# Attention with a two-layer FFN: the second layer summed in six PSUM banks over a pair of token tiles, the first layer's block products in two

## The chip, the core and the metric

The kernel runs on one core of a Trainium2 chip. The metric is the device time of one execution in microseconds; before the change its median over three runs is 757.24 us (756.86 to 758.57).

## What is computed

Attention for 4 batches, 8 heads, 576 positions and head size 64, with a bias from a small network on the log of the distance; then an FFN over the 2304 tokens.

```python
scores = q @ k^T / 8 + bias(rel. position)
attn   = softmax(scores);  x = (attn @ v)            # -> 2304 x 512
h = x @ w_in                                          # 512 -> 2048
g = maximum(0.01 * h, h)
out = g @ w_out                                       # 2048 -> 512
```

`w_in` and `w_out` arrive as float64. The kernel gets them as pairs of 32-bit words and builds float32 from the bits on the chip.

## The kernel before

The program has two stages, both with an order of work written out by hand (`manual_schedule`): each engine takes its instructions strictly in the order in which the Python code emits them, and waits on semaphores that the framework puts in. So a waiting instruction holds up all that is emitted behind it on its engine.

**Attention** is a sequence of 16 units (two heads of one batch), each of nine tiles: `step(n)` issues scores (TensorE), softmax (DVE and ScalarE), transposes and the product with v. In fixed slots of each unit (L577) it also takes one operation from `early_ops`: the weights of the FFN are cut in 16 chunks `m`, each with a half of `w_in` (h = 0) and a half of `w_out` (h = 1), and one half is assembled by `w_abs` (ScalarE, absolute value of the raw word) and four `w_bits` (DVE). A raw half is 512 KB; `w_fill` issues its load on SP's queue as soon as one of the `raw` buffers is free, and a buffer becomes free at the fourth `w_bits` of its half. `EARLY` chunks are assembled in attention, the rest in the first pair of the FFN, from the list `conv`, where each half's four `w_bits` are followed by the `w_abs` of the half after next.

**The FFN** runs over 24 periods `g`: three pairs of 384-token tiles (`p`), each with eight groups `m` of two weight chunks. The period `g` computes the first layer of its group with seven block products instead of eight, after Winograd: `prod(g, j)` multiplies a sum of blocks of `w_in` (`w1b`, built by `s_sum`, `w1_hi`, `w1_lo`) with a sum of blocks of x (`xo`, built by `x_sum`, `x_hi`, `x_lo`). Every operand is split into a high part in the fast format and a rest (`_hi` on ScalarE, `_lo` a subtraction), and a product is six matmuls of 384 columns: high by high, high by rest and rest by high, for two halves of the contraction. `keep` (ScalarE) and `comb` (DVE) add the products in `c` tiles to the four blocks of h; `relu` (two ScalarE operations) and `g_lo` make the high part and the rest of g. Later groups keep their built weights in DRAM: `w1_out` writes 1792 KB in the first pair, `w1_in` reads them back in the two others.

In the same period `l2(g-1, q)`, q = 0 to 5, multiplies the previous group's g with `w_out` (`ws`, built by `w2_split`), six matmuls of 512 columns each, in a bank of tag `o`; `flush` then adds the bank to the result in `xa`, on DVE, and after the pair's last group sends the rows out. The order on TensorE in one period is: products 0 and 1, l2 0, product 2, l2 1, product 3, l2 2, product 4, l2 3, l2 4, products 5 and 6, l2 5.

PSUM has eight banks: tag `s` has two tiles of two banks each, tags `t` and `o` two tiles of one bank. Products 0 and 1 share one `s` tile, 2 and 3 the other, 4 to 6 take turns in `t`, and l2 has `o`.

```python
def prod(g, j):
    if j in (0, 2):
        t = pstile("s")
        bank[g, j], bank[g, j + 1] = t[:, 0:HT], t[:, 512:512 + HT]
    elif j > 3:
        bank[g, j] = pstile("t")[:, 0:HT]
```

GpSimd does `s_sum`, `w1_lo`, the rest part of `w2_split`, `x_sum`, and `g_lo` for blocks 0 and 3; DVE does `g_lo` for blocks 1 and 2, the flushes and the assembly of weights. `work(budget)` puts, at four places of a period, some of the waiting weight operations into the order: first those of `todo` (next group's weights), then `conv`, until the given costs are used up.

Of the kernel before, what the change touches and what calls it, by code (L numbers as in the profile page):

```python
# [8 lines left out]
F32 = mybir.dt.float32  # L9
# [14 lines left out]
KW = 2 * S + 64  # L24
EARLY = 9
RING = 7
HT = 384
NG = MF // 2
# [12 lines left out]
def attention_ffn(ctx: ExitStack, tc: tile.TileContext, qt, kt, vm, vt, wi, wo, cst, out):  # L41
# [330 lines left out]
    pools, y1, y2, raws, w1b, ws, st_, xt = {}, {}, {}, {}, {}, {}, {}, {}  # L372
    free, nxt = [3], [0]

    def w_fill():
        while nxt[0] < 2 * MF and free[0]:
            p = nxt[0]
            free[0] -= 1
            t = pools["raw"].tile([128, DM, 2], I32, tag="raw", name="raw", bufs=3)
# [50 lines left out]

    def w1_lo(g, k):
        s, y = w1_src(g, k)
        w = w1b[g % 2]
        nc.gpsimd.tensor_sub(w[:, 1, s], y, w[:, 0, s].bitcast(F32))
        if k == 2:
            del y1[2 * g], y1[2 * g + 1]
# [7 lines left out]
    def w1_ops(g):  # L444
        l = [(0.01, s_sum, g, k) for k in range(4)]
        for k in range(3):
            l += [((0.65, 0.36, 1.05)[k], w1_hi, g, k), (0, w1_lo, g, k)]
        return l + [(0, w1_out, g)]

# [14 lines left out]
    def x_sum(p, o):  # L464
        t = pools["raw"].tile([128, DM, 2], I32, tag="raw", name="raw", bufs=3) if p else pools["fp"].tile([128, 2, DM], F32, tag="ws", name="ws", bufs=4)
# [8 lines left out]
    def x_hi(p, o):  # L474
        x_new(p, o)
        nc.scalar.copy(out=xo[p, o][:, 0], in_=x_of(p, o))
# [3 lines left out]

    bank, gt, gf, ct, flush_q = {}, {}, {}, {}, []

    def prod(g, j):
        if j in (0, 2):
            t = pstile("s")
            bank[g, j], bank[g, j + 1] = t[:, 0:HT], t[:, 512:512 + HT]
        elif j > 3:
            bank[g, j] = pstile("t")[:, 0:HT]
        w, x = w1b[g % 2], xo[g // NG, j]
        n = 0  # L490
        for k in range(2):
            c = slice(128 * k, 128 * k + 128)
            for a, b in ((0, 0), (0, 1), (1, 0)):
                nc.tensor.matmul(bank[g, j], w[:, a, PROD[j], c], x[:, b, k, :], start=(n == 0), stop=(n == 5))  # L494
                n += 1

    def c_new(g, c):
        ct[g, c] = pools["fp"].tile([128, HT], F32, tag="c", name="c", bufs=6)
# [16 lines left out]
    def g_lo(g, c):  # L515
        t = gt[g, c]
        (nc.vector if c in (1, 2) else nc.gpsimd).tensor_sub(t[:, 1], gf.pop((g, c))[:], t[:, 0].bitcast(F32))  # L517

    def l2(g, q):
        tk = (q + 3) % 6  # L520
        o = pstile("o")
        n = 0
        for i in range(2):
            t, w = gt[g, 2 * i + tk // 3], ws[2 * g + i]
            c = slice(128 * (tk % 3), 128 * (tk % 3) + 128)
            for a, b in ((0, 0), (0, 1), (1, 0)):
                nc.tensor.matmul(o[:], t[:, a, c], w[:, b], start=(n == 0), stop=(n == 5))  # L527
                n += 1
        flush_q.append((g, tk, o))

    def flush():
        if not flush_q:
            return
        g, tk, o = flush_q.pop(0)
        p, m = divmod(g, NG)
        t0 = 2 * HT * p
        y = xa[tk // 3][:, :, t0 + 256 * (tk % 3):t0 + 256 * (tk % 3) + 256]
        o = o[:].rearrange("p (a c) -> p a c", a=2)
        if m:
            nc.vector.tensor_add(y, o, y)  # L540
        else:
            nc.vector.tensor_copy(y, o)
        if m == NG - 1:
            t0 += 128 * tk
            nc.sync.dma_start(out=out[t0:t0 + 128, :].rearrange("t (a c) -> t a c", a=2), in_=y)

    with tc.manual_schedule():
# [6 lines left out]
        for n in range(NTILE + LAG + 6):  # L554
# [15 lines left out]
            if n == 13:  # L570
                w_fill()
                for m in range(EARLY):
                    for h in range(2):
                        early_ops += [(w_abs, m, h)] + [(w_bits, m, h, k) for k in range(4)]
                    if m == 1:
                        early_ops += [f[1:] for f in w1_ops(0)]
            for _ in range({0: 3, 4: 3, 8: 1}.get(i, 0) if n >= 14 else 0):  # L577
                if early_ops:
# [18 lines left out]
        fp.tile([128, HT], F32, tag="gf", name="gf", bufs=2)  # L597
        fp.tile([128, HT], F32, tag="c", name="c", bufs=6)
        for m in range(EARLY, MF):
            y2[m] = fp.tile([128, DM], F32, name=f"y2_{m}")  # L600
        for o in (0, 1):
            x_hi(0, o)
            x_lo(0, o, nc.gpsimd)
        for o in (3, 2, 4, 6):
            x_sum(0, o)
        for o in (2, 3, 4, 5, 6):
            x_hi(0, o)
        for o in (2, 3, 4, 5, 6):
            x_lo(0, o, nc.vector)

        halves_ = [(m, i) for m in range(EARLY, MF) for i in range(2)]
# [5 lines left out]
        todo = []  # L617

        def work(budget):
            for l, left in ((todo, 0.8), (conv, budget)):  # L620
                while l and left > 0 and (l[0][1] != w_abs or l[0][3] or len(y1) < RING):
                    cost, f, *args = l.pop(0)
                    f(*args)
                    left -= cost

        G = NG * NPAIR
        for g in range(G + 1):
            p, m = divmod(g, NG)
            a, b = g < G, g > 0
            last = m == NG - 1 and p + 1 < NPAIR  # L630
            todo += [(0.62, w2_split, 2 * g + i) for i in range(2)] if a else []
            if g + 1 < NG:
                while any(t[1:4] == (w_bits, 2 * g + 3, 0) for t in conv):
                    conv[0][1](*conv.pop(0)[2:])
                todo += w1_ops(g + 1)
            elif g + 1 < G:
                w1_in(g + 1)
            if m == NG - 2 and p + 1 < NPAIR:
                todo += [(0, x_hi, p + 1, 0), (0.93, x_lo, p + 1, 0, nc.vector)]

# [11 lines left out]

            def xs(f, *o):
                if last:
                    for i in o:
                        f(p + 1, i)

            def xl(*o):
                if last:
                    for i in o:  # L660
                        x_lo(p + 1, i, nc.vector)

            pr(0)
            do(keep)
            pr(1)
            flush()
            xs(x_sum, 3)
            xs(x_hi, 1)
            lt(0)
            pr(2)  # L670
            do(comb, 2, 2, 0)
            do(comb, 0, 1, 0)
            do(relu, 0)
# [36 lines left out]
            xs(x_hi, 5, 6)  # L710
            xl(4)
            work(0.6)
            do(g_lo, 1)
            do(g_lo, 2)
            xl(5, 6)
            while todo:
                work(0)
            if g == NG - 2:
                assert not conv
            if not a:  # L720
                while flush_q:
                    flush()

# [41 lines left out]
```

## Time and profile before

| what | before |
|---|---|
| median of 3 runs | 757.24 us |
| time of the profiled execution | 760.83 us |
| its span, first to last instruction | 759.0 us |
| TensorE busy | 695.9 us (92%) |
| DVE busy | 546.6 us (72%) |
| ScalarE busy | 405.8 us (53%) |
| GpSimd busy | 312.7 us (41%) |
| mean granted TensorE clock | 0.973 |

The profiled execution's time is 3.6 us above the median of the runs; its span is 1.8 us above it. A span in the rows below is counted in microseconds from the first instruction. Busy time of TensorE has modelled ends, so that a busy TensorE need not be at its peak; the view of one period's chain shows what each product takes when nothing holds it.

Attention ends near 304 us. The FFN's first product starts there; its first pair (periods 0 to 7) takes until about 472, the second until 602 and the third to the end.

### The profile page before, as it was taken

Reading aid. Unit: us, or ns where it says so; the run is one execution under the profiler, and the core shown is the slowest. Engines: PE = TensorE matmul, PEld = TensorE weight load, DVE = VectorE, ACT = ScalarE, POOL = GpSimd, SP = SyncE. Lnnn points to the kernel's source line nnn. Section 1 sums busy time; section 2 is a strip of 40 time slices with the busy share of each in tenths; the row PEclk is TensorE's granted clock in tenths of the full one; section 3 lists DMA queues with packets and bytes.
Section 4 is the critical chain, followed back from the end, with each engine's and each line's share of the span. In section 5 each row is a group of like instructions: output and inputs, shape, how many; then the busy total and the mean of one; then the engine's idle time right before and its main releaser. Section 6 shows DMA issues by size and latency. Waiting matters only on the chain.

```text
span 759.0 us, 11958 instructions
## 1 busy us (share of the span) xinstructions
PE 695.9 (92%) x4240; PEld 560.0 (74%) x4240; DVE 546.6 (72%) x1112; ACT 405.8 (53%) x874; POOL 312.7 (41%) x297
## 2 busy tenths in 40 slices
PE   7999999999999999468888888899999989999997
PEld 3446787787877777457677677788888878888886
DVE  8986888788988896548989969554555765554554
ACT  8996877787787787343344443332233432332331
POOL 0023436554343441566777776222223632222231
PEclk9999999999999999789999999899999999999999
DMA  9987685687479511024343316343322234333202
GB/s 241 352 275 198 186 249 144 204 222 208 136 204 237 160 57 56 0 97 153 140 173 122 143 66 223 128 141 156 113 98 97 98 134 143 106 144 140 97 2 83
DMA packets 36028, 112.35 MB, mean 148 GB/s; under 512 B 8576, under 2 KB 13312, under 8 KB 32896
## 3 DMA queue, kind: packets, MB, share of 16 engines
q1 hardware_dynamic: 35968, 111.59, 45.9%
q8 instruction: 33, 0.54, 0.3%
q14 instruction: 27, 0.22, 0.1%
HBM read 81.28 MB, written 30.29 MB: 147 GB/s over the span
## 4 chain that ended last, share of the span: by engine, by line
PE 48%; DVE 9%; ACT 4%; POOL 3%; issue 3%; ACTq 0%; POOLq 0%; DVEq 0%
PE ps_o L527 21%; PE ps_s L494 13%; PE ps_t L494 7%; PE ps_o L346 2%; DVE c L506 2%; PE ps_s L246 2%; PE ps_t L311 2%; DVE x L540 2%; ACT c L502 1%; DVE y L398 1%; POOL ws L469 1%; DVE y L400 1%; DVE xo L479 1%; DVE y L396 1%; ACT g L512 1%
## 5 line engine op out<-in xcount | busy, mean ns | idle before, releaser
L527 PE MATMUL ps_o<-ws,g 128*128 128x512 f32 x864 | 226.7, 403 | 11.8 <-DVE x L540 7.4
L527 PEld LDWEIGHTS ps_o<-ws,g 128*128 128x128 f32 x864 | 163.7, 193 | 43.8 <-DVE x L540 8.4
L512 ACT ACTIVATE g<-c 128x384 fp32r<-128x384 f32 x96 | 50.3, 524 | 244.8 <-DVE c L506 240.8
L453 POOL TENSOR_TENSOR ws<-y,ws 128x512 fp32r<-128x512 f32 x48 | 65.0, 1375 | 233.5 <-ACT ws L452 228.0
L269 DVE CUSTOM_DVE_ANT_0 p<-ps_s,bias 128x576 f32<-128x576 f32 x128 | 95.0, 751 | 24.0 <-PE ps_s L246 18.6
L277 ACT ACTIVATE p<-p,mx 128x576 f32<-128x576 f32 x128 | 99.7, 779 | 9.8 <-DVE mx L269 7.7
L506 DVE TENSOR_TENSOR c<-ps_s,c 128x384 f32<-128x384 f32 x72 | 40.1, 557 | 88.8 <-PE ps_s L494 88.0
L540 DVE TENSOR_TENSOR x<-ps_o,x 128x512 f32<-128x512 f32 x126 | 86.1, 684 | 20.5 <-PE ps_o L527 20.4
L327 ACT COPY PT<-ps_t 128x512 f32<-128x512 f32 x128 | 73.7, 576 | 43.6 <-PE ps_t L311 43.6
L246 PE MATMUL ps_s<-ks,qs 128*128 128x288 f32 x480 | 93.7, 317 | 1.8 <-DVE mx L269 1.8
L494 PE MATMUL ps_s<-xo,w1a 128*128 128x384 f32 x288 | 63.5, 359 | 23.5 <-ACT c L502 22.8
L246 PEld LDWEIGHTS ps_s<-ks,qs 128*128 128x128 f32 x480 | 67.6, 189 | 15.6 <-issue 7.4
L494 PEld LDWEIGHTS ps_s<-xo,w1a 128*128 128x128 f32 x288 | 54.6, 202 | 31.6 <-ACT c L502 26.7
L311 PE MATMUL ps_t<-ident,p 128*128 128x128 f32 x512 | 77.5, 274 | 0.0
L494 PE MATMUL ps_s<-xo,w1c 128*128 128x384 f32 x288 | 62.1, 350 | 15.1 <-ACT c L502 10.5
L211 POOL TENSOR_TENSOR qs<-raw,qs 64x512 fp32r<-64x512 f32 x30 | 37.8, 1281 | 89.6 <-DVE qs L199 75.5
L346 PE MATMUL ps_o<-PT,v 128*64 128x288 f32 x512 | 69.2, 412 | 0.9 <-DVE PT L301 0.9
L494 PEld LDWEIGHTS ps_s<-xo,w1c 128*128 128x128 f32 x288 | 52.3, 194 | 23.0 <-ACT c L502 14.5
L311 PEld LDWEIGHTS ps_t<-ident,p 128*128 128x128 f32 x512 | 61.1, 140 | 9.0 <-issue 8.2
L506 DVE TENSOR_TENSOR c<-ps_t,c 128x384 f32<-128x384 f32 x96 | 50.5, 551 | 21.6 <-PE ps_t L494 21.6
L517 POOL TENSOR_TENSOR g<-gf,g 128x384 fp32r<-128x384 f32 x48 | 53.0, 1104 | 2.4 <-ACT gf L513 2.4
L287 POOL COPY rb<-sm 128x256 f32<-128x256 f32 x32 | 14.4, 450 | 94.8 <-DVE sm L284 94.8
(106 smaller groups left out, 1130.4 us busy)
## 6 DMA issues: line engine op xcount, KB each, us to landing
w1a<-w SPq DMA_DIRECT2D x8, 1792.0 KB, 7.4
w1c<-w SPq DMA_DIRECT2D x8, 1792.0 KB, 7.4
raw<-kt SPq DMA_DIRECT2D x32, 304.0 KB, 6.0
raw<-qt SPq DMA_DIRECT2D x32, 288.0 KB, 4.5
raw<-wi SPq DMA_DIRECT2D x16, 512.0 KB, 3.7
raw<-wo SPq DMA_DIRECT2D x16, 512.0 KB, 4.0
w<-w1a SPq DMA_DIRECT2D x4, 1792.0 KB, 5.7
w<-w1c SPq DMA_DIRECT2D x4, 1792.0 KB, 6.6
```

The costliest lines, as they stand in the source:

```text
L246: nc.tensor.matmul(s_[:, S0 + HS * hh:S0 + HS * hh + HS], qs[:, c0:c0 + 128], ks[:, k0 + HS * hh:k0 + HS * hh + HS], start=(j == 0), stop= ...
L269: nc.vector.tensor_tensor_reduce(out=p, in0=s_[:, S0:S0 + S], in1=bt, scale=-0.125, scalar=3.4e38, op0=ALU.add, op1=ALU.min, accum_out=i)
L277: nc.scalar.activation(out=p, in_=p, func=AF.Exp, bias=i, scale=-1.0, accum_out=sm)
L311: nc.tensor.transpose(t0[:, 128 * jb:128 * jb + 128], p[:, p0 + 128 * jb:p0 + 128 * jb + 128], ident[:])
L327: nc.scalar.copy(out=PT[:, g, 0:8, c].rearrange("p (j h) c -> p j h c", h=2)[:, :, h, :], in_=t0[:].rearrange("p (j c) -> p j c", j=4))
L346: nc.tensor.matmul(o[64 * h:64 * h + 64, 0:HS], l, r, start=(jb == 0), stop=(jb == 4))
L453: nc.gpsimd.tensor_sub(t[:, 1], y2[c % MF][:], t[:, 0].bitcast(F32))
L494: nc.tensor.matmul(bank[g, j], w[:, a, PROD[j], c], x[:, b, k, :], start=(n == 0), stop=(n == 5))
L506: nc.vector.tensor_add(a if c == src else c_new(g, c), bank[g, j], a)
L512: nc.scalar.activation(out=t[:, 0], in_=h, func=AF.Prelu, alpha=0.01)
L527: nc.tensor.matmul(o[:], t[:, a, c], w[:, b], start=(n == 0), stop=(n == 5))
L540: nc.vector.tensor_add(y, o, y)
```

## The change

- `l2` no longer has a bank of its own for each use. In a pair it keeps six banks: both `s` tiles (q = 0 to 3) and both `o` tiles (q = 4, 5), and accumulates there over the pair's eight groups. `flush` is gone; after the pair's last group each bank is copied out once, by DVE for even q and by ScalarE for odd q.
- All products take turns in the two `t` banks, except in the very first period, where they take `s`, `s`, `o`, `o`, `t`, `t`, `s`.
- The order on TensorE in a period becomes strictly alternating from product 1 on: products 0 and 1, l2 0, product 2, l2 1, product 3, l2 2, product 4, l2 3, product 5, l2 4, product 6, l2 5.
- Ten chunks are assembled in attention instead of nine, with one slot more in each unit, and group 1's `s_sum` too; the rest of group 1's weights is built before the first period. `conv` starts with period 1 and has six chunks.
- The `raw` buffers are two instead of three; the `y1` ring has eight tiles, `c` eight.
- `g_lo` of all blocks and `w1_lo` (but for groups 0 and 1) go from GpSimd to DVE. At the start of the FFN the first two `x_lo` go to DVE as well, and GpSimd starts with `x_sum`.
- The next group's weight work has fixed places in the period (`todo[0]` to `todo[5]`), and `conv` gets budgets of 1.2, 0.6, 1.2, 0, 0.6 and 1.2.

The diff, cut to its core:

```diff
-EARLY = 9
-RING = 7
+EARLY = 10
+RING = 8
+RAWS = 2
...
-    free, nxt = [3], [0]
+    free, nxt = [RAWS], [0]
...
     def prod(g, j):
-        if j in (0, 2):
-            t = pstile("s")
-            bank[g, j], bank[g, j + 1] = t[:, 0:HT], t[:, 512:512 + HT]
-        elif j > 3:
-            bank[g, j] = pstile("t")[:, 0:HT]
+        o = bank[g, j] = pstile("ssoott"[j % 6] if g == 0 else "t")[:, 0:HT]
...
     def keep(g):
-        nc.scalar.copy(out=c_new(g, 0), in_=bank[g, 0])
+        nc.scalar.copy(out=c_new(g, 2), in_=bank[g, 0])
...
-        (nc.vector if c in (1, 2) else nc.gpsimd).tensor_sub(t[:, 1], gf.pop((g, c))[:], t[:, 0].bitcast(F32))
+        nc.vector.tensor_sub(t[:, 1], gf.pop((g, c))[:], t[:, 0].bitcast(F32))
 
     def l2(g, q):
+        p, m = divmod(g, NG)
         tk = (q + 3) % 6
-        o = pstile("o")
+        if m == 0:
+            if q in (0, 2):
+                t = pstile("s")
+                acc[p, q], acc[p, q + 1] = t[:, 0:512], t[:, 512:1024]
+            elif q > 3:
+                acc[p, q] = pstile("o")[:]
+        o = acc[p, q]
...
-                nc.tensor.matmul(o[:], t[:, a, c], w[:, b], start=(n == 0), stop=(n == 5))
+                nc.tensor.matmul(o, t[:, a, c], w[:, b], start=(m == 0 and n == 0), stop=(m == NG - 1 and n == 5))
...
-        if m:
-            nc.vector.tensor_add(y, o, y)
-        else:
-            nc.vector.tensor_copy(y, o)
         if m == NG - 1:
+            t0 = 2 * HT * p
+            y = xa[tk // 3][:, :, t0 + 256 * (tk % 3):t0 + 256 * (tk % 3) + 256]
+            o = o.rearrange("p (a c) -> p a c", a=2)
+            if q % 2:
+                nc.scalar.copy(out=y, in_=o)
+            else:
+                nc.vector.tensor_copy(y, o)
...
-            for _ in range({0: 3, 4: 3, 8: 1}.get(i, 0) if n >= 14 else 0):
+                early_ops += [(s_sum, 1, k) for k in range(4)]
+            for _ in range({0: 3, 4: 3, 6: 1, 8: 1}.get(i, 0) if n >= 14 else 0):
...
-        for o in (0, 1):
-            x_hi(0, o)
-            x_lo(0, o, nc.gpsimd)
+        for o in range(7):
+            x_new(0, o)
         for o in (3, 2, 4, 6):
             x_sum(0, o)
-        for o in (2, 3, 4, 5, 6):
+        for o in (0, 1, 5, 3, 2):
             x_hi(0, o)
-        for o in (2, 3, 4, 5, 6):
+        for o in range(4):
             x_lo(0, o, nc.vector)
+        for k in range(3):
+            w1_hi(1, k)
+            w1_lo(1, k, nc.gpsimd)
+        w1_out(1)
...
+        def conv_some(left):
+            while conv and left > 0 and (conv[0][1] != w_abs or conv[0][3] or len(y1) < RING):
+                cost, f, *args = conv.pop(0)
+                f(*args)
+                left -= cost
...
+                todo[0] += [(s_sum, g + 1, k) for k in range(4)]
+                for k in range(3):
+                    todo[k + 1] += [(w1_hi, g + 1, k), (w1_lo, g + 1, k, nc.vector)]
+                todo[4].append((w1_out, g + 1))
...
+            def work(k, left):
+                for f, *args in todo[k]:
+                    f(*args)
+                if g:
+                    conv_some(left)
 
             pr(0)
             do(keep)
             pr(1)
+            do(comb, 0, 1, 2)
+            work(0, 1.2)
             lt(0)
+            do(relu, 0)
             pr(2)
+            do(comb, 2, 2, 2)
+            do(g_lo, 0)
+            work(1, 0.6)
             lt(1)
             pr(3)
             do(comb, 1, 3, 2)
+            work(2, 1.2)
             lt(2)
             pr(4)
             do(comb, 3, 4, 1)
             do(comb, 2, 4, 2)
+            work(3, 0)
             lt(3)
             do(relu, 3)
+            pr(5)
+            do(comb, 1, 5, 1)
+            do(g_lo, 3)
             lt(4)
+            do(relu, 1)
+            work(4, 0.6)
             pr(6)
             do(comb, 2, 6, 2)
+            do(g_lo, 1)
             lt(5)
             do(relu, 2)
+            work(5, 1.2)
             do(g_lo, 2)
```

## Rows read from the trace of the kernel before

**Rows 1.** Windows by stage: start:end, length; busy (count) by engine; PEclk, DMA share, GB/s

```profile
85.00:293.00 208.00, 207.74 (x1668) 161.37 (x1665) 175.78 (x458) 164.98 (x376) 93.14 (x109) 1.00 0.64 178
304.00:334.30 30.30, 14.34 (x56) 12.33 (x55) 13.93 (x16) 12.15 (x22) 20.63 (x16) 0.74 0.02 8
334.30:433.80 99.50, 84.29 (x385) 71.80 (x384) 88.29 (x121) 41.81 (x82) 69.39 (x55) 0.96 0.40 149
496.10:595.00 98.90, 95.49 (x469) 84.18 (x469) 54.01 (x91) 32.41 (x68) 31.70 (x26) 1.00 0.31 115
```

**Rows 2.** Chain that ended last, one period of the second pair: start, length, what

```profile
512.55 1.31 PE ps_s L494 x6
513.86 1.39 PE ps_o L527 x6
...
527.42 1.06 PE ps_s L494 x6
...
528.50 0.49 ACT c L502
...
529.03 0.97 PE ps_s L494 x4
```

**Rows 3.** Waits, whole run: who waited for whom, us, times, longest

```profile
PE ps_s L494 <- ACT c L502: 33.3, 24, 9.2
```

**Rows 4.** Groups of the page: line, engine, operation, shapes, count | busy, mean ns | idle before

```profile
L506 DVE TENSOR_TENSOR c<-ps_t,c 128x384 f32<-128x384 f32 x96 | 50.5, 551 | 21.6 <-PE ps_t L494 21.6
L540 DVE TENSOR_TENSOR x<-ps_o,x 128x512 f32<-128x512 f32 x126 | 86.1, 684 | 20.5 <-PE ps_o L527 20.4
```

**Rows 5.** Timeline by engine, start of the FFN: start, length, engine, what [idle before]

```profile
304.04 1.31 PE L494 MATMUL ps_s<-xo,w1a 128*128 128x384 f32 x6
314.52 4.21 PE L494 MATMUL ps_s<-xo,w1a 128*128 128x384 f32 x12 [9.17 <-ACT c L502]
334.31 2.29 PE L527 MATMUL ps_o<-ws,g 128*128 128x512 f32 x6
304.14 0.46 DVE L351 TENSOR_TENSOR x<-ps_o,PT 128x288 f32<-128x288 f32 x1 [2.83 <-PE ps_o L346]
309.89 5.03 DVE L479 TENSOR_TENSOR xo<-ws,xo 128x768 fp32r<-128x768 f32 x3 [5.29 <-ACT xo L476]
314.84 0.95 DVE L479 TENSOR_TENSOR xo<-x,xo 128x768 fp32r<-128x768 f32 x1
305.31 1.80 POOL L469 TENSOR_TENSOR ws<-x 128x768 f32<-128x768 f32 x1
```

**Rows 6.** Timeline of DVE and GpSimd, end of period 5: an assembly, and a lone pair

```profile
435.15 0.41 DVE L394 TENSOR_SCALAR y<-y 128x512 f32<-128x512 f32 x1
...
436.79 0.69 DVE L400 SCALAR_TENSOR_TENSOR y<-raw,y 128x512 int32<-128x512 int32 x1
...
432.07 2.69 DVE L517 TENSOR_TENSOR g<-gf,g 128x384 fp32r<-128x384 f32 x1
...
431.53 2.81 POOL L434 TENSOR_TENSOR w1a<-sum,w1a 128x1024 fp32r<-128x1024 f32 x1
```

**Rows 7.** Raw loads, 300 to 500 us (landing), SP's timeline, ScalarE's timeline

```profile
DMA to landing us min/median/max: 3.4/3.5/7.5
...
374.80 0.33 SPq L439 DMA_DIRECT2D w<-w1c  x1
375.21 0.38 SPq L380 DMA_DIRECT2D raw<-wo  x1
...
382.70 0.68 ACT L388 ACTIVATE y<-raw 128x512 f32<-128x512 f32 x1 [0.55 <-DMA raw<-wo]
```

**Rows 8.** Timeline of TensorE after a long wait: start, length, what [idle before]

```profile
476.99 2.29 PE L494 MATMUL ps_s<-xo,w1a 128*128 128x384 f32 x6 [3.45 <-ACT c L502]
```

**Rows 9.** Timeline, end of the run: last l2 products and the last flush

```profile
747.90 7.09 PE L527 MATMUL ps_o<-ws,g 128*128 128x512 f32 x30 [0.16 <-DVE x L540]
...
755.03 0.69 DVE L540 TENSOR_TENSOR x<-ps_o,x 128x512 f32<-128x512 f32 x1 [0.67 <-PE ps_o L527]
```

More of the change, by code (lines that the diff above doesn't have):

```diff
@@ L378, in w_fill @@
             free[0] -= 1
-            t = pools["raw"].tile([128, DM, 2], I32, tag="raw", name="raw", bufs=3)
+            t = pools["raw"].tile([128, DM, 2], I32, tag="raw", name="raw", bufs=RAWS)
             nc.sync.dma_start(out=t[:].rearrange("p c t -> p (c t)"), in_=(wi, wo)[p % 2][64 * (p - p % 2):64 * (p - p % 2) + 128, :].bitcast(I32))
@@ L442, in w1_in @@
         nc.sync.dma_start(out=w1b[g % 2][:].rearrange("p t s c -> p (t s c)").bitcast(F32), in_=wscr[g % NG][:])
[L444 to L448, printed above, removed]
     def w2_split(c):
@@ L464, in x_sum @@
     def x_sum(p, o):
-        t = pools["raw"].tile([128, DM, 2], I32, tag="raw", name="raw", bufs=3) if p else pools["fp"].tile([128, 2, DM], F32, tag="ws", name="ws", bufs=4)
+        if p == 0:
+            t = pools["fp"].tile([128, 2, DM], F32, tag="ws", name="ws", bufs=4)
+        elif o == 4:
+            t = pools["early"].tile([128, 4, 256], F32, tag="sum", name="sum", bufs=1)
+        else:
+            t = pools["raw"].tile([128, DM, 2], I32, tag="raw", name="raw", bufs=RAWS)
         xt[p, o] = t[:].rearrange("p a b -> p (a b)")[:, 0:2 * HT].bitcast(F32).rearrange("p (a c) -> p a c", a=2)
@@ L474, in x_hi @@
     def x_hi(p, o):
-        x_new(p, o)
         nc.scalar.copy(out=xo[p, o][:, 0], in_=x_of(p, o))
@@ L493, in prod @@
             for a, b in ((0, 0), (0, 1), (1, 0)):
-                nc.tensor.matmul(bank[g, j], w[:, a, PROD[j], c], x[:, b, k, :], start=(n == 0), stop=(n == 5))
+                nc.tensor.matmul(o, w[:, a, PROD[j], c], x[:, b, k, :], start=(n == 0), stop=(n == 5))
                 n += 1
     def c_new(g, c):
-        ct[g, c] = pools["fp"].tile([128, HT], F32, tag="c", name="c", bufs=6)
+        ct[g, c] = pools["fp"].tile([128, HT], F32, tag="c", name="c", bufs=8)
         return ct[g, c][:]
     def keep(g):
-        nc.scalar.copy(out=c_new(g, 0), in_=bank[g, 0])
+        nc.scalar.copy(out=c_new(g, 2), in_=bank[g, 0])
     def comb(g, c, j, src):
@@ L575, in attention_ffn @@
                     if m == 1:
-                        early_ops += [f[1:] for f in w1_ops(0)]
-            for _ in range({0: 3, 4: 3, 8: 1}.get(i, 0) if n >= 14 else 0):
+                        early_ops += [(s_sum, 0, k) for k in range(4)]
+                        for k in range(3):
+                            early_ops += [(w1_hi, 0, k), (w1_lo, 0, k, nc.gpsimd)]
+                        early_ops.append((w1_out, 0))
+                early_ops += [(s_sum, 1, k) for k in range(4)]
+            for _ in range({0: 3, 4: 3, 6: 1, 8: 1}.get(i, 0) if n >= 14 else 0):
                 if early_ops:
@@ L616, in attention_ffn @@
                 conv.append((0, w_abs, *halves_[j + 2]))
[L617 to L624, printed above, removed]
+        def conv_some(left):
[3 more added lines that the diff above has]
+                left -= cost
         G = NG * NPAIR
@@ L630, in attention_ffn @@
             last = m == NG - 1 and p + 1 < NPAIR
-            todo += [(0.62, w2_split, 2 * g + i) for i in range(2)] if a else []
-            if g + 1 < NG:
-                while any(t[1:4] == (w_bits, 2 * g + 3, 0) for t in conv):
-                    conv[0][1](*conv.pop(0)[2:])
-                todo += w1_ops(g + 1)
-            elif g + 1 < G:
+            todo = [[] for _ in range(6)]
+            if a:
+                todo[0].append((w2_split, 2 * g))
+                todo[2].append((w2_split, 2 * g + 1))
+            if 0 < g and g + 1 < NG:
+                while any(t[1:4] == (w_bits, 2 * g + 3, 0) for t in conv):
+                    _, f, *args = conv.pop(0)
+                    f(*args)
+                todo[0] += [(s_sum, g + 1, k) for k in range(4)]
+                for k in range(3):
+                    todo[k + 1] += [(w1_hi, g + 1, k), (w1_lo, g + 1, k, nc.vector)]
+                todo[4].append((w1_out, g + 1))
+            elif NG <= g + 1 < G:
                 w1_in(g + 1)
             if m == NG - 2 and p + 1 < NPAIR:
-                todo += [(0, x_hi, p + 1, 0), (0.93, x_lo, p + 1, 0, nc.vector)]
+                todo[4] += [(x_new, p + 1, 0), (x_hi, p + 1, 0), (x_lo, p + 1, 0, nc.vector)]
+            if last:
+                n = p + 1
+                todo[0] += [(x_sum, n, 3), (x_sum, n, 2), (x_new, n, 1), (x_hi, n, 1)]
+                todo[1] += [(x_new, n, 2), (x_lo, n, 1, nc.vector), (x_sum, n, 4)]
+                todo[2] += [(x_new, n, 3), (x_hi, n, 2), (x_hi, n, 3), (x_lo, n, 2, nc.vector)]
+                todo[3] += [(x_new, n, 4), (x_new, n, 5), (x_sum, n, 6), (x_lo, n, 3, nc.vector), (x_hi, n, 4)]
+                todo[4] += [(x_new, n, 6), (x_hi, n, 5), (x_lo, n, 4, nc.vector)]
+                todo[5] += [(x_hi, n, 6), (x_lo, n, 5, nc.vector), (x_lo, n, 6, nc.vector)]
+            if g == 0:
+                todo[1].append((x_lo, 0, 4, nc.vector))
+                todo[2].append((x_lo, 0, 5, nc.vector))
+                todo[3].append((x_lo, 0, 6, nc.vector))
             def pr(j):
@@ L651, in lt @@
                     l2(g - 1, q)
[L653 to L661, printed above, removed]
+            def work(k, left):
+                for f, *args in todo[k]:
+                    f(*args)
+                if g:
+                    conv_some(left)
             pr(0)
```

58 lines of the change are left out of this document (7 added, 51 removed).

## The prediction, made before the changed kernel ran

> **What bounds the kernel now.** I read the windows by stage first [rows 1]. In attention (85 to 293 us) TensorE is busy 207.74 of 208.00 us and DVE 175.78: TensorE sets the pace and DVE has 15% to spare. At the start of the FFN (304 to 334.3) TensorE has 14.34 busy of 30.30 us, partly at half clock (granted mean 0.74). In the first pair (334.3 to 433.8, five periods of 19.9 us) it has 84.29 of 99.50 and DVE 88.29: DVE sets the pace there. In the second pair (496.1 to 595, six periods of 16.48) it has 95.49 of 98.90. So there are three different losses.
>
> Next I read the chain of a steady period [rows 2]. From product 1 (512.55) to the next period's product 1 (529.03) are 16.48 us: products of 1.05, l2 blocks of 1.39, and one stop: product 0 starts at 527.42 and takes 1.06, but product 1 starts at 529.03, right after `keep` (528.50, 0.49), because products 0 and 1 share a tile. That costs 529.03 - 528.48 = 0.55, and 1.31 - 1.05 = 0.26 more for a product that starts from a standstill: 0.81 us a period; the waits show it in all 24 periods [rows 3].
>
> **Part by part.**
>
> *Steady periods.* Each product now has a bank of its own, so product 1 no longer waits: 16.48 - 0.81 = 15.67 us. What is late next? Two banks in turn mean that product j waits for the readers of product j-2. In the new order, from product 0 at 0, products start at 0, 1.05, 3.49, 5.93, 8.37, 10.81, 13.25 and the next period at 15.7. A reader starts 0.2 after a product's end and takes 0.49 (`keep`) or 0.55 per `comb` [rows 2, 4]. The narrowest places are product 0 to 2 (keep done at 1.75, needed at 3.49) and product 6 to the next product 1 (comb done at 15.1, needed at 16.74); l2 0 needs `g_lo`(1) at 17.8, done at 15.7. All have 1.6 us or more. DVE loses 126 + 18 flushes of 0.684 [rows 4], some 98 us, and gets 9 copies (ScalarE the other 9) and 48 more `g_lo`; that lies beside TensorE and counts nothing.
>
> *Attention.* The tenth chunk brings two halves: four DVE operations of 2.3 us together [rows 6] and one 0.7 on ScalarE [rows 7] each, and four GpSimd sums. DVE has 32 us to spare in this stage [rows 1]; in sequence it could cost between 0 and 4.6. I take 1, nearer to cover.
>
> *First period.* Before, GpSimd made two `x_lo` and only then four `x_sum` from 305.31 on, at 1.80 each; product 1 started at 314.52 after 9.17 idle, and the first l2 block at 334.31 [rows 5]. Now GpSimd starts its sums right after attention, near 299, and ends near 307. DVE is held by its last attention step until 304.6 [rows 5]; then `x_lo` 0 to 3, between 0.95 and 1.68 each (alone, or the three beside GpSimd in 5.03) [rows 5]: to 308.4 or 311.3; I take 311. Then come, in DVE's order, two combs, g_lo(0), `x_lo` 4, comb, `x_lo` 5, two combs, `x_lo` 6, with products 4, 5 and 6 each behind its `x_lo`: 311 + 6 x 0.55 + 3 x 0.95 = 317.2, and product 6 ends at 318.2 (319.9 if TensorE is at half clock, where six matmuls take 2.1 instead of 1.05 [rows 5]). With attention's 1, period 1 starts at 320; its l2 0 then starts near 322, 12 us sooner than before.
>
> *Periods 1 to 5, with the raw loads.* DVE's work per period: 7 combs and 4 g_lo at 0.55, `w1_lo` some 2.2 (estimated from 0.95 for 768 columns, for 1792), 12 halves in 4.6 periods at 2.3: 14.2 at most of 15.67, plus waits on GpSimd. So throughput would do. But `raw` has two buffers now. In `conv` a half's fourth `w_bits` frees a buffer, only then SP issues the load of the half after next, and the very next entry is that half's `w_abs` on ScalarE. With three buffers the load had a half's time of lead; now none. A load lands 3.5 us after its issue, and 7.5 if it leaves behind a `w1_out` (issued 375.21 behind 374.80, read at 382.70; 7.9 after the `w1_out`) [rows 7]. ScalarE stands in that time, and with it all that is queued behind: `relu`, `w1_hi` or `keep`; behind `relu` and `w1_hi` stand `g_lo` and `w1_lo` on DVE, behind `keep` product 2. Ten of the twelve halves are concerned (A2 to A11).
>
> Counting the budgets through: period 1 emits A2 in `work(2)`, A3 in `work(5)`; period 2 A4 in `work(0)`, ahead of relu(0), A5 in `work(2)`, A6 in `work(5)`; period 3 A7 and A8; period 4 A9, A10, and A11 in `work(5)`. Period 1 from its product 0: half 0 ends on DVE at 7.9, its successor lands at 11.5, A2 ends 12.1, `w1_hi`(2) about 13.1, `w1_lo`(2) 14.3, the comb of product 5 at 14.85, needed at 15.7: hidden. Half 1 ends at 16.0; `w1_out` left at 14.4, so the load lands at 22.3, A3 ends 22.9, `keep` of period 2 at 23.4, where product 2 was due at 19.2: TensorE stands 4.2 us. Walked on like that, A6 and A11 stop `keep` by 4.3 and 4.4; A4 and A5 hold DVE by 3 us each, and TensorE loses 4.5 of it in products 5, 6 and the next 0; A7, A9 and A10 together 3.3. After a stop of 3.45 us the clock was at half, a product taking 2.29 instead of 1.06 [rows 8]; most of that falls where DVE is late anyhow, 2.5 us count. Sum: 5 x 15.67 + 12.9 + 4.5 + 3.3 + 2.5 = 101.6 us, no better than the 99.5 of before [rows 1]. Period 6 starts at 421.6.
>
> The Trainium skill's page "DMA: Bandwidth & Descriptors" (Rules for kernel authors) says to issue a DMA early and wait on its semaphore late. It speaks against the third buffer's removal, as the rows do.
>
> The Trainium skill's page "SBUF — State Buffer" (Who interferes with whom) says that a DVE instruction with two SBUF inputs and a GpSimd instruction that reads SBUF lock each other out for the whole instruction. By that each `g_lo` and `w1_lo` now on DVE can still stand behind one of GpSimd's six operations per period.
>
> On that the trace shows a lone `g_lo` of 2.69 us beside a GpSimd subtraction of 2.81 [rows 6], against some 0.55 for its size. GpSimd had 69.39 of 99.50 us busy there [rows 1] and keeps about 5.5 a period; I have put 0.5 to 0.7 into each of three places of a period for it, bounds 0 and 1.8.
>
> *Periods 6 to 23.* 18 x 15.67 = 282.1, to 703.7. The work on x before pairs 2 and 3 fits: the last `x_lo` ends before its product, and the copies have 1.05 us (a product) before the tile's other half is written.
>
> *End.* Six l2 blocks take 7.1 + 1.2 before them = 8.3; a copy now stands between q = 0 and 1 and between 2 and 3, which share tiles: 2 x 0.95. From the last l2 (754.99) to the span's end were 4.0, copy and sending [rows 9]; that stays. 703.7 + 8.3 + 1.9 + 4.0 = 717.9. The span of before is 759.0, 1.8 above the median, so the time is 716.
>
> **The rivals.** (A) *The raw loads are hidden*, because a `w_abs` lands where ScalarE has slack. The 23.2 us of stops and slow clock fall away: 693. For it: before, only one `w_abs` ever waited, 0.55 us [rows 7]. Against: that was with a buffer more. 22%.
>
> (B) *The loads stand in full and decide: slower than before.* Place: `w_abs` in ScalarE's queue; every half then runs in sequence, load, `w_abs`, bits. Price: ten times 7.5 + 0.7 instead of the 23 counted, 716 + 59 = 775. It ends above 757 when the mean loss per load is over (41 + 23) / 10 = 6.4 us. Only loads behind a `w1_out` showed over 3.5 [rows 7]; 6%.
>
> (C) *The stop of 0.81 comes back elsewhere.* If DVE, now with all `g_lo`, frees a product's bank later than the margin of 1.6 us, each steady period loses about what it won: 18 x 0.81 = 14.6, 731. The same size follows if GpSimd's locks cost TensorE 2.9 us in each of periods 1 to 5. 12%.
>
> (D) *The change gains nothing*: l2 stays in PSUM by its code, but if attention loses 4.6 and (B) takes two thirds of its price, 716 + 3.6 + 39 = 759 comes out, and somewhat less at a little under that. 3%.
>
> **How the numbers follow.** Forecast 716 (704 to 727): 57%; A 22%, C 12%, B 6%, D 3%. The range that leaves out no more than 2 in 10 takes in most of A, the bounds of attention and of the first period, and C: 691 to 740. About 0.2% (1.5 us) is what a measurement of this kernel can tell from no change. Faster: 57 + 22 + 12 + 2 of D = 93%; same 1%; slower 6%.
>
> **What would show it.** Steady periods of 15.7 to 15.8 us with no wait of product 1 for `keep`; the first l2 block near 322 instead of 334.3; ScalarE's `w_abs` (L388) waiting for DMA some ten times, over 20 us in all, and TensorE waiting for `keep` (L502) by over 4 us at three period starts of the first pair. If L388 waits little and the periods 1 to 5 take 16 us, A holds. If steady periods are above 16, the two-bank margins were wrong. If DVE is busy without gaps in periods 1 to 5, the locks or its work and not the loads bound them.

## The result, and the profile after

The changed kernel takes 747.19 us (median of four runs, 745.10 to 749.14) against 757.16 (four runs too, one more than in the table of before): a ratio of 0.9864 (95% interval 0.9835 to 0.9894). That is a gain of 1.4%, small but clear of the spread; it is 31 us above the forecast and outside the range of 691 to 740. The profiled execution took 749.14 us with a span of 747.4, where the prediction's sum had come to a span of 717.9.

| stretch of the span | predicted | after | miss |
|---|---|---|---|
| attention's last DVE step starts | 305.1 | 323.25 | 18.1 |
| from there to period 1's first product | 14.9 | 17.53 | 2.7 |
| periods 1 to 5 | 101.6 | 108.0 | 6.4 |
| period 6 to the end | 296.3 | 298.6 | 2.3 |

The four misses make 29.5 us, the whole distance of the spans. Periods 1 to 5 are measured from `keep` to `keep`, and the last row is what then remains of the span. (The times are some 1.6 us further apart than the spans: the prediction took 1.8 us off its span, and here the median lies 0.2 below the span.)

The windows of the changed kernel (start:end, length; busy (count) of TensorE, its weight loads, DVE, ScalarE, GpSimd; granted clock, DMA share, GB/s) stand against [rows 1]:

```profile
85.00:293.00 208.00, 199.71 (x1577) 152.82 (x1573) 179.11 (x440) 158.41 (x357) 94.92 (x105) 1.00 0.65 181
342.42:450.45 108.03, 89.53 (x390) 76.45 (x389) 77.46 (x119) 42.08 (x83) 33.44 (x30) 0.89 0.37 134
529.55:607.00 77.45, 77.45 (x387) 69.54 (x386) 37.67 (x58) 29.94 (x59) 21.92 (x14) 1.00 0.32 116
```

The last line is the gain that was meant: in steady periods TensorE is busy without a gap. The first is a loss that was not: in attention TensorE had 207.74 of 208.00 us, and has 199.71 now. The second is periods 1 to 5, from `keep` to `keep`: 18.5 us without work, and a mean granted clock of 0.89. The window of [rows 1] beside it, 99.50 us, runs from the first l2 block of period 1 to product 1 of period 6. From `keep` to `keep` the kernel before took 101.59 us for these periods, so the change made them 6.4 us longer:

```profile
331.72 0.45 ACT L502 COPY c<-ps_s 128x384 f32<-128x384 f32 x1
433.31 0.46 ACT L502 COPY c<-ps_s 128x384 f32<-128x384 f32 x1
```

The waits of the whole run (who waited for whom: us, times, longest) name the two losses. Before, ScalarE's softmax waited 7.7 us for DVE's `mx`, and one `w_abs` waited 0.55 us for a load [rows 7]:

```profile
ACT p L278 <- DVE mx L270: 26.3, 43, 2.6
ACT y L389 <- DMA raw<-wo: 26.1, 5, 6.5
ACT y L389 <- DMA raw<-wi: 24.1, 6, 7.8
...
PE ps_t L489 <- ACT c L497: 13.1, 3, 5.7
```

The wait for `keep` has shrunk from 24 times [rows 3] to 3. The timeline of ScalarE shows `keep` of two neighbouring steady periods, 15.64 us apart:

```profile
513.91 0.48 ACT L497 COPY c<-ps_t 128x384 f32<-128x384 f32 x1 [0.80 <-PE ps_t L489]
529.55 0.48 ACT L497 COPY c<-ps_t 128x384 f32<-128x384 f32 x1 [0.80 <-PE ps_t L489]
```

And the start of the FFN, the answer to [rows 5]:

```profile
322.27 1.82 POOL L469 TENSOR_TENSOR ws<-x,x 128x768 f32<-128x768 f32 x1
323.25 0.46 DVE L352 TENSOR_TENSOR x<-ps_o,PT 128x288 f32<-128x288 f32 x1 [2.83 <-PE ps_o L347]
323.63 3.78 DVE L478 TENSOR_TENSOR xo<-x,xo 128x768 fp32r<-128x768 f32 x2
327.33 3.43 DVE L478 TENSOR_TENSOR xo<-ws,xo 128x768 fp32r<-128x768 f32 x2
333.35 2.02 DVE L478 TENSOR_TENSOR xo<-ws,xo 128x768 fp32r<-128x768 f32 x1
335.76 1.58 DVE L478 TENSOR_TENSOR xo<-x,xo 128x768 fp32r<-128x768 f32 x1
340.78 2.27 PE L489 MATMUL ps_t<-xo,w1c 128*128 128x384 f32 x12
342.89 1.31 PE L530 MATMUL ps_s<-ws,g 128*128 128x512 f32 x5
```

### The profile page after: what moved, and what is told of

Same layout as the page of the kernel before. It is cut to its first block, busy times and chain, and to the rows that moved or that the text cites. A ratio compares the mean times of both kernels' runs of the same rounds, so it can differ in the third digit from the quotient of the medians.

```text
span 747.4 us, 11823 instructions
## 1 busy us (share of the span) xinstructions
PE 697.6 (93%) x4240; PEld 561.5 (75%) x4240; DVE 502.5 (67%) x1045; ACT 412.5 (55%) x883; POOL 238.1 (32%) x229
## 4 chain that ended last, share of the span: by engine, by line
PE 41%; DVE 11%; DMA 5%; ACT 5%; issue 3%; DVEq 0%; ACTq 0%; SPq 0%
PE ps_t L489 17%; PE ps_s L530 13%; PE ps_o L530 7%; DMA raw<-wo 3%; DVE xo L478 2%; DMA raw<-wi 2%; DVE c L501 2%; PE ps_o L347 2%; DVE y L401 1%; DVE g L513 1%; ACT y L389 1%; ACT p L278 1%; DVE p L270 1%; DVE y L399 1%; PE ps_t L312 1%
## 5 line engine op out<-in xcount | busy, mean ns | idle before, releaser
L501 DVE TENSOR_TENSOR c<-ps_t,c 128x384 f32<-128x384 f32 x164 | 88.8, 554 | 144.6 <-PE ps_t L489 129.1
L530 PE MATMUL ps_s<-ws,g 128*128 128x512 f32 x576 | 152.5, 401 | 2.5 <-DVE x L539 2.5
L530 PEld LDWEIGHTS ps_s<-ws,g 128*128 128x128 f32 x576 | 109.1, 192 | 21.5 <-DVE x L539 4.0
L489 PE MATMUL ps_t<-xo,w1c 128*128 128x384 f32 x504 | 104.2, 346 | 12.4 <-ACT c L497 8.5
L489 PEld LDWEIGHTS ps_t<-xo,w1c 128*128 128x128 f32 x504 | 93.1, 195 | 21.0 <-ACT c L497 9.3
L489 PE MATMUL ps_t<-xo,w1a 128*128 128x384 f32 x474 | 97.1, 342 | 8.6 <-ACT c L497 4.7
L489 PEld LDWEIGHTS ps_t<-xo,w1a 128*128 128x128 f32 x474 | 85.4, 191 | 18.0 <-ACT c L497 5.1
L513 DVE TENSOR_TENSOR g<-gf,g 128x384 fp32r<-128x384 f32 x96 | 63.3, 659 | 17.5 <-ACT gf L509 17.5
L530 PE MATMUL ps_o<-ws,g 128*128 128x512 f32 x288 | 74.2, 393 | 0.0
L530 PEld LDWEIGHTS ps_o<-ws,g 128*128 128x128 f32 x288 | 53.4, 188 | 8.5
```

What stands on the lines that cost most here:

```text
L489: nc.tensor.matmul(o, w[:, a, PROD[j], c], x[:, b, k, :], start=(n == 0), stop=(n == 5))
L513: nc.vector.tensor_sub(t[:, 1], gf.pop((g, c))[:], t[:, 0].bitcast(F32))
L530: nc.tensor.matmul(o, t[:, a, c], w[:, b], start=(m == 0 and n == 0), stop=(m == NG - 1 and n == 5))
```

## The experiments

Times are medians of four runs, ratios are to the kernel before on the same chip; before itself took 757.65 to 758.34 us beside them. The changed kernel's 747.19 was measured beside a before of 757.16, so a difference to it is good to some 2 us.

### Where attention lost 19 us

The changed kernel's timeline in attention, at the slot in tile 6 that the change adds:

```profile
246.16 3.39 POOL L215 TENSOR_TENSOR ks<-raw,ks 128x576 fp32r<-128x576 f32 x2
...
246.18 1.97 DVE L401 SCALAR_TENSOR_TENSOR y<-raw,y 128x512 int32<-128x512 int32 x1
248.07 0.74 DVE L270 CUSTOM_DVE_ANT_0 p<-ps_s,bias 128x576 f32<-128x576 f32 x1
...
248.87 0.80 PE L247 MATMUL ps_s<-ks,qs 128*128 128x288 f32 x4 [0.84 <-DVE mx L270]
248.91 0.78 ACT L278 ACTIVATE p<-p,mx 128x576 f32<-128x576 f32 x1 [1.22 <-DVE mx L270]
```

GpSimd starts the two subtractions of the key split at 246.16; the `w_bits` that starts on DVE at 246.18 takes 1.97 us instead of 0.69 [rows 6], the softmax step queued behind it is late, and ScalarE and TensorE wait for it. The trace has ten such `w_bits` of 1.62 to 1.97 us in attention, the kernel before none. Theory "place": it is this neighbour that costs, 10 x 1.27 = 13 us. Rival "number": ten more DVE operations, wherever they stand, no longer fit.

**The slot moved, in the changed kernel** (tile 8 takes two operations, tile 6 none):

```diff
-            for _ in range({0: 3, 4: 3, 6: 1, 8: 1}.get(i, 0) if n >= 14 else 0):
+            for _ in range({0: 3, 4: 3, 8: 2}.get(i, 0) if n >= 14 else 0):
```

> The changed kernel, with the slot that it adds to each attention unit moved from tile 6 to tile 8 (tile 8 then takes two operations); the number of operations is the same. In the changed kernel attention's last step on DVE ends at 323.7 us instead of 304.6 before. Theory (place): at tile 6 a weight operation on DVE runs beside GpSimd's split of the keys and is held by it (one took 1.97 us there instead of 0.69), and the next softmax with it. Then attention's last step comes back to 305 to 309 and the time falls by 14 to 18 us, to about 731. Rival (number): the ten operations more of the tenth chunk are too many for DVE wherever they stand; then the last step stays at 318 or later and the time at 742 to 747.

Measured: 737.31 us, ratio 0.9728 (0.9688 to 0.9768), 10 us below the changed kernel. In attention no `w_bits` takes over 0.93 us any more, a fourth one 0.76, and DVE's timeline has the last step 13 us sooner:

```profile
245.99 0.76 DVE L401 SCALAR_TENSOR_TENSOR y<-raw,y 128x512 int32<-128x512 int32 x1
...
310.26 0.46 DVE L352 TENSOR_TENSOR x<-ps_o,PT 128x288 f32<-128x288 f32 x1 [2.83 <-PE ps_o L347]
```

Both numbers lie between those that the two theories had named. How much of the 13 us is the place's shows in other profiles of the same attention code: with the slot at tile 6 (the runs with the later `w_abs` and without the loads, below) the last step starts at 319.35 and 320.96, with the slot at tile 8 (both edits together, below) at 310.24. So the place is worth 9 to 13 us of span, and 10 in the medians. Some 4 to 6 us against the kernel before stay.

```profile
319.35 0.46 DVE L352 TENSOR_TENSOR x<-ps_o,PT 128x288 f32<-128x288 f32 x1 [2.83 <-PE ps_o L347]
```

**One operation moved to tile 6, in the kernel before** (as many operations as before):

```diff
-            for _ in range({0: 3, 4: 3, 8: 1}.get(i, 0) if n >= 14 else 0):
+            for _ in range({0: 2, 4: 3, 6: 1, 8: 1}.get(i, 0) if n >= 14 else 0):
```

> The kernel before, with one of the three weight operations of tile 0 moved to tile 6; the number per unit stays seven. Theory (place): attention gets longer by 10 to 18 us although it does the same work, and the time is 767 to 775. Rival (number): nothing is added, the time stays within 2 us of 757.

Measured: 769.29 us, ratio 1.0134 (1.0083 to 1.0186), slower with the same work: 11 us. Nine `w_bits` of 1.70 to 1.97 us are there (9 x 1.27 = 11 us), and attention ends 13.5 us later than before:

```profile
317.62 0.46 DVE L351 TENSOR_TENSOR x<-ps_o,PT 128x288 f32<-128x288 f32 x1 [2.83 <-PE ps_o L346]
```

**The neighbour taken away, in the changed kernel** (the slot in tile 6 stays):

```diff
-            nc.gpsimd.tensor_sub(ks2[:, c], k_[:, c], ks1[:, c].bitcast(F32))
+            pass
...
-        for j, ks in enumerate((ks1, ks2)):
+        for j, ks in enumerate((ks1, ks1)):
```

> The changed kernel without GpSimd's subtraction that makes the rest part of the keys in attention; the high part is used in its place, so the scores lack the keys' rest. The slots stay as the change has them. If w_bits at tile 6 is slow because it stands beside this subtraction, and DVE's softmax steps late through it, attention's last step comes back to 304 to 309 and the time to 729 to 735. If it is only the number of DVE operations in tiles 6 to 8, whatever runs beside them, the last step stays at 318 or later and the time above 742.

Measured: 734.41 us, ratio 0.9692 (0.9654 to 0.973); attention's last step at 307.60, 15.6 us sooner. The groups of DVE in attention (busy us, mean ns), first of the changed kernel, then of this one, have the same twenty operations of the second and third kind at 554 and 896 ns and at 427 and 703:

```profile
L399 DVE SCALAR_TENSOR_TENSOR y<-raw,y 128x512 int32<-128x512 int32 x20 | 17.9, 896 | 0.3
...
L397 DVE TENSOR_SCALAR y<-y 128x512 int32<-128x512 int32 x20 | 11.1, 554 | 0.3
```

```profile
L399 DVE SCALAR_TENSOR_TENSOR y<-raw,y 128x512 int32<-128x512 int32 x20 | 14.1, 703 | 0.3
...
L397 DVE TENSOR_SCALAR y<-y 128x512 int32<-128x512 int32 x20 | 8.5, 427 | 0.3
```

With the three runs, place is shown: the same operations cost some 10 us more at tile 6 than at tile 8 or 0, and no longer do when GpSimd's subtraction is gone. The number costs the rest, some 4 to 6 us. (Attention code like that of the kernel before ended between 303.94 and 306.43 us in four kernels of this study, and that of the changed kernel between 319.35 and 323.25 in three, so single microseconds are not to be read here.)

### What the raw loads cost

The chain of the changed kernel that ended last, periods 2 to 5 (start, length, what):

```profile
376.82 0.62 DVE y L401
377.49 3.44 DMA raw<-wo
380.95 0.66 ACT y L389
...
386.28 0.60 DVE y L401
386.90 4.42 DMA raw<-wi
391.34 0.66 ACT y L389
392.00 0.38 ACT c L497
...
425.27 0.61 DVE y L401
425.90 7.85 DMA raw<-wo
433.77 0.66 ACT y L389
434.43 0.38 ACT c L497
434.85 2.29 PE ps_t L489 x6
437.13 2.48 PE ps_s L530 x6
439.62 1.06 PE ps_t L489 x6
```

It is the sequence that the prediction described: a half's fourth `w_bits` (L401), the load that it releases, that load's `w_abs` (L389), and `keep` (L497) behind it; loads of 3.4 to 4.4 us, and 7.85 behind a `w1_out` that SP had issued at 424.37. Nine of the ten loads of periods 1 to 5 lie on this chain, 40.8 us together, and no work of TensorE between 341 and 434.85. Rival to the loads: DVE's own work, or the two banks, set these periods.

**The loads left out, in the changed kernel** (from half 22 on the two last raw tiles are read again):

```diff
+            if p >= 2 * EARLY + 2:
+                raws[p // 2, p % 2] = kept[p % 2]
+                nxt[0] += 1
+                continue
...
-            raws[p // 2, p % 2] = t
+            raws[p // 2, p % 2] = kept[p % 2] = t
```

> The changed kernel, in which the loads of the last ten raw halves are left out and the two last raw tiles are read again, so the weights of the last five chunks are wrong. Everything else is as in the change. If the raw loads are what stretches periods 1 to 5, these go from 108 to 78 to 88 us, ScalarE's waits for DMA in the FFN from 48 to under 3, and the time is 717 to 727. If DVE or the two banks bound these periods, they keep over 100 us and the time stays above 740.

Measured: 719.21 us, ratio 0.9495 (0.9454 to 0.9536). The window of periods 1 to 5:

```profile
340.17:420.62 80.45, 79.81 (x390) 69.25 (x389) 78.51 (x119) 41.88 (x83) 34.66 (x30) 1.00 0.25 106
```

The periods go from 108.03 to 80.45 us, so the loads cost 27.6. TensorE's busy time falls with them, from 89.53 to 79.81 for the same 390 records: of the 27.6, 17.9 are idle time and 9.7 are slower matmuls. (That divides TensorE's time and not the cause, since the chain above reaches TensorE only at 434.85.) DVE is busy 78.51 of 80.45, and half of the chain that ended last there is its own: without the loads it is DVE that keeps these periods at 16.1 instead of 15.64. In each of them one `w_bits` takes 1.69 to 1.78 us instead of 0.69 beside a subtraction of GpSimd.

**The order changed, the loads kept** (each `w_abs` comes three `w_bits` later, still with two buffers):

```diff
-            conv += [(0.42, w_bits, *t, 0), (0.43, w_bits, *t, 1), (0.69, w_bits, *t, 2), (0.69, w_bits, *t, 3)]
-            if j + 2 < len(halves_):
-                conv.append((0, w_abs, *halves_[j + 2]))
+            conv += [(0.42, w_bits, *t, 0), (0.43, w_bits, *t, 1), (0.69, w_bits, *t, 2)]
+            if 0 < j and j + 1 < len(halves_):
+                conv.append((0, w_abs, *halves_[j + 1]))
+            conv.append((0.69, w_bits, *t, 3))
```

> The changed kernel, with each w_abs of the first pair emitted behind the third instead of ahead of the first w_bits of the half before its own; buffers, loads and work are the same. Theory (raw loads): ScalarE's w_abs waits for DMA for 48 us in the first pair, and the periods 1 to 5 take 108 us for it. With three bits of lead the waits fall under 15 us, the periods 1 to 5 take 84 to 92, and the time is 724 to 731. Rival (DVE's work or GpSimd's locks bound the periods): they stay over 100 us and the time over 740.

Measured: 723.52 us, ratio 0.9545 (0.9509 to 0.9581); ScalarE's waits for loads 18.5 us instead of 50.2 (16.7 of them in the first pair, a little over the 15 expected), periods 1 to 5 in 85.52, clock 1.00:

```profile
338.91:424.43 85.52, 80.48 (x391) 69.26 (x390) 74.48 (x119) 41.75 (x83) 33.58 (x30) 1.00 0.45 161
```

So it is not the loads' bandwidth but the place of the wait for them: 22.5 us come back with every byte still moved.

### Both together, and the parts apart

**The slot at tile 8 and the later `w_abs`**, both edits above.

> Both edits together: the added slot at tile 8 and the later w_abs. If the two losses are separate they add up: attention's last step at 305 to 309, periods 1 to 5 in 84 to 92 us, the time 706 to 714. If one hides behind the other the time stays over 720.

Measured: 713.71 us, ratio 0.9423 (0.9384 to 0.9462). The gains add: 9.9 and 23.7 apart, 33.5 together. So the two losses are separate.

**The FFN's part of the change alone:**

```diff
-EARLY = 10
-RING = 8
-RAWS = 2
+EARLY = 9
+RING = 7
+RAWS = 3
...
-                early_ops += [(s_sum, 1, k) for k in range(4)]
-            for _ in range({0: 3, 4: 3, 6: 1, 8: 1}.get(i, 0) if n >= 14 else 0):
+            for _ in range({0: 3, 4: 3, 8: 1}.get(i, 0) if n >= 14 else 0):
...
+        for k in range(4):
+            s_sum(1, k)
```

> The changed kernel, with attention's part of the change undone: nine chunks in attention in the old slots, group 1's s_sum after attention, three raw buffers, rings of seven and six c tiles; the FFN's new order, its banks and its fixed places stay, and conv has seven chunks now. If the loss lies in the slot at tile 6 and in the second buffer, both are gone: attention's last step at 304 to 306 instead of 323, ScalarE's waits for raw loads under 15 us instead of 50, the first period some 2 us longer by the four sums, seven chunks instead of six over periods 1 to 5 or 6 at 16 to 17 us; time 700 to 715. If the third buffer gives nothing (w_abs stands behind the same loads, since the order of emission is what delays them), the waits stay above 35 us and the time is 725 to 735. If attention stays late without the slot, its last step is above 315.

Measured: 708.96 us, ratio 0.9358 (0.9318 to 0.9397). Attention is as before, and seven chunks in the FFN cost less than six did with two buffers (windows of attention and of periods 1 to 5):

```profile
85.00:293.00 208.00, 207.72 (x1666) 161.50 (x1663) 175.74 (x459) 164.91 (x376) 93.16 (x109) 1.00 0.63 178
326.86:410.83 83.97, 80.25 (x391) 69.42 (x390) 78.69 (x122) 42.95 (x85) 33.17 (x30) 1.00 0.46 168
```

The tenth chunk in attention was to spare the FFN work; what came with it (the slot beside the key split, two raw buffers instead of three, group 1's `s_sum` in attention, deeper rings) cost 38 us in all. This run does not part them.

**The stop at product 1 alone, in the kernel before** (products 0 and 2 in one tile, 1 and 3 in the other; the flushes stay):

```diff
-        if j in (0, 2):
+        if j < 2:
...
-            bank[g, j], bank[g, j + 1] = t[:, 0:HT], t[:, 512:512 + HT]
+            bank[g, j], bank[g, j + 2] = t[:, 0:HT], t[:, 512:512 + HT]
```

> The kernel before, with one thing changed: products 0 and 2 share one tile of two banks, 1 and 3 the other, so that product 1 no longer stands behind keep. If that stop is worth 0.81 us in each steady period, as the prediction has it, the periods of the second and third pair take 15.7 us instead of 16.5, and 16 to 20 of the 24 gain: time 741 to 745. If the stop comes back elsewhere (the banks of tag o behind flush, product 3 behind comb), the periods stay above 16.2 and the time above 750.

Measured: 739.60 us, ratio 0.9761 (0.9724 to 0.9798), a little more gain than expected. Two indices bring more than the whole change did. The windows, five periods of the first pair and six of the second:

```profile
332.14:431.78 99.64, 85.35 (x394) 71.06 (x393) 90.43 (x123) 41.74 (x83) 70.44 (x56) 0.98 0.41 151
489.08:584.09 95.01, 95.01 (x470) 84.02 (x469) 53.92 (x91) 32.36 (x68) 31.65 (x26) 1.00 0.34 120
```

The second pair's periods take 15.83 us. Twelve such periods gain 7.8 us, and the four around the two pair starts another 8.2. The first pair's take 19.93, from `keep` to `keep`, where the kernel before took 20.32, and DVE is busy 90.43 of 99.64: there this edit hardly helps. With the FFN's part alone, which has no flushes, DVE has 78.69 there. Against that run 30.6 us are left for the flushes' removal and the rest of the new order; the runs don't divide them further.

**The FFN's part with the later `w_abs`**, and with the run's last six l2 blocks in an order in which no copy stands between two that share a tile:

```diff
-                    l2(g - 1, q)
+                    l2(g - 1, q if a else (0, 2, 4, 1, 3, 5)[q])
```

> The FFN-only version (nine chunks in attention, three raw buffers) with two more things: each w_abs follows its half's predecessor by one more operation (it is put ahead of that half's fourth w_bits, so its load has had most of a half longer to land), and the run's last six l2 blocks go in the order q = 0, 2, 4, 1, 3, 5, so that no copy stands between two that share a tile. If the last waits for raw loads (12 us on ScalarE) are the rest of what the first pair loses, periods 1 to 5 go from 84 to about 80 us and the loads' waits under 4; the end is 1.6 to 1.9 us shorter; time 702 to 706. If the FFN's start and DVE hold the first pair, periods 1 to 5 stay at 83 to 84, and only the end is gained: 707.

Measured: 705.11 us, ratio 0.9307 (0.9248 to 0.9365), the best of the study. Periods 1 to 5 take 81.71 us, ScalarE waits 3.4 us for loads in them, and from the last `keep` to the end of the span are 26.6 us instead of 28.9. Its interval overlaps that of the FFN's part alone, so the gain between the two is seen in the traces rather than in the times.

## Why the prediction was wrong, step by step

**The failed step is attention: "DVE has 32 us to spare in this stage", cost 1, bounds 0 to 4.6.** It was 19.1 in the profiled execution, and 15 to 17 in two others with the same attention code. The 32 us were a sum over 208; what counts is the place of an operation, ahead of which softmax step and beside which GpSimd instruction it stands. The row that priced it was at hand: a lone `g_lo` of 2.69 us beside a GpSimd subtraction of 2.81 [rows 6]. The prediction weighed it for the `g_lo` and `w1_lo` of the FFN, and did not ask the same of the one slot in attention that was new. Without that neighbour the cost would have lain about the upper bound: with the slot at tile 8 attention still ends 4 to 6 us later than before.

The Trainium skill's page "SBUF — State Buffer" (Who interferes with whom) says of a DVE instruction in a two-port mode that whoever issues first gets the shared ports for the whole instruction and the other is fully blocked, and of one with two SBUF inputs that it contends with a GpSimd instruction that reads SBUF. The traces agree: GpSimd starts at 246.16 and DVE at 246.18, and each of the ten operations, `TENSOR_SCALAR` or `SCALAR_TENSOR_TENSOR`, takes 1.2 to 1.3 us more.

**Steady periods: right.** 15.67 predicted, 15.64 measured; no wait for `keep`, and the margins of the two banks held. Rival C did not come. With only the tiles rearranged the period is 15.83, so 0.65 of the 0.84 us that a period won is the stop, as the sum had it.

**First period: right in kind, 2.7 us short.** `x_lo` 0 to 3 took 3.78 + 3.43 = 7.2 us instead of 6.4, `x_lo` 4 and 5 took 2.02 and 1.58 instead of 0.95 each, all beside GpSimd: 2.5 us. `x_lo` 6, with no GpSimd work beside it, took 0.95. It is the same mis-sizing by the same neighbour, as the timeline shows it; no run was made for it.

**Periods 1 to 5: the mechanism right, the size 6.4 us short.** The stops of `keep` came in the three periods named (A3, A6 and A11 delay periods 2, 3 and 5) and TensorE waited 13.1 us there, 12.9 predicted; `w_abs` waited ten times in the FFN. Rival A is out, since the loads cost 27.6 us. Rival B had the place right, load, `w_abs` and `w_bits` in sequence on the chain, but not the price: slower than before needed 6.4 us lost for each load, and it was 2.8.

The Trainium skill's page "DMA: Bandwidth & Descriptors" (Rules for kernel authors) says to issue a transfer early and to wait on it late. The later `w_abs` agrees: 22.5 us for a later wait.

Two terms were short. Without the loads the five periods take 80.45, where the sum began at 78.35: DVE, with a `w_bits` held beside GpSimd in each of them, is 2.1 us behind the pace. The loads' terms, 12.9 + 4.5 + 3.3 + 2.5 = 23.2, measured 27.6, 4.4 more. How these 4.4 us divide stays open. TensorE waited 5.2 us for `comb` where 7.8 were expected, and its matmuls took 9.7 us longer where 2.5 were to count, but a slow matmul and a wait for DVE can stand in for each other. "Most of that falls where DVE is late anyhow" held behind the first two stops, where the chain goes on through DVE and the next load. Behind the third TensorE is the late one, and there a product and an l2 block took 2.3 us longer (2.29 and 2.48 instead of 1.06 and 1.39), near the 2.5 of the sum.

The comparison with before in that sum, 101.6 against 99.5, used the window of [rows 1], which leaves out 2.1 us; from `keep` to `keep` the forecast was no change for these periods.

**Period 6 to the end: 2.3 us short,** 1.3 up to the last `keep`, where the two pair starts took 17.0 us each instead of 15.67 and the periods behind them a little less, and 1.0 behind it.

With both losses undone the kernel takes 713.71, near the forecast of 716. That is no merit of the forecast: the loads' 23 were in it.

## What to carry to other kernels

Spare time of an engine, summed over a stage, does not price an added instruction: look at what runs on the neighbour engine at the very slot, and at what is queued behind it. A buffer taken away is paid by the wait that stood behind its lead; moving the consumer later in its queue gave back 23 us with two buffers. When a change frees one engine and loads another stage, run its parts apart: here one part was worth some 49 us and the other cost 38.

## What the hardware showed that was not expected

A DVE operation with a single SBUF input was held as long as one with two: the `TENSOR_SCALAR` forms took 1.70 us (one 1.62) instead of 0.43, the `SCALAR_TENSOR_TENSOR` forms 1.97 instead of 0.69, about 1.27 more each. The softmax step, which reads PSUM and SBUF, was not: 0.74 to 0.76 with and without the neighbour. The changed kernel's timeline, then that of the run with the slot at tile 8:

```profile
113.53 3.12 POOL L215 TENSOR_TENSOR ks<-raw,ks 128x576 fp32r<-128x576 f32 x2
113.55 1.70 DVE L395 TENSOR_SCALAR y<-y 128x512 f32<-128x512 f32 x1
```

```profile
251.17 2.95 POOL L215 TENSOR_TENSOR ks<-raw,ks 128x576 fp32r<-128x576 f32 x2
251.19 0.75 DVE L270 CUSTOM_DVE_ANT_0 p<-ps_s,bias 128x576 f32<-128x576 f32 x1
```

Behind the stops of this run the clock was slow for a while. In TensorE's own account slower matmuls took half as much as the idle time (9.7 against 17.9 us, above); on the chain they lay only behind the longest stop. The windows of the changed kernel around it:

```profile
428.50:434.80 6.30, 0.63 (x3) 0.19 (x1) 0.30 (x1) 1.03 (x3) 0.00 (x0) 0.82 0.47 147
434.80:439.60 4.80, 4.75 (x13) 4.20 (x14) 4.74 (x7) 2.79 (x6) 4.13 (x4) 0.52 0.00 0
439.60:450.50 10.90, 10.90 (x57) 9.84 (x56) 8.60 (x13) 3.92 (x8) 3.14 (x3) 1.00 0.40 168
```

After 6.30 us with 0.63 of work the granted clock was 0.52, near the 1.2 GHz level, in a stretch in which TensorE was busy 4.75 of 4.80 us; then it was 1.00 again, at 2.4 GHz. The six matmuls of a product took 2.29 us there and 1.04 to 1.06 later, and in the three kernels whose waits for loads were shorter (windows above) the clock is 1.00 over the five periods.
